# Buffers of the first weights' decoding moved off the first block's tiles, new planner costs, gates of the MLPs on two engines, and the first two blocks of the second MLP interleaved

## The chip, the cores and the metric

One core of one Trainium2 chip runs the whole program. The metric is the device time of one execution in microseconds (us), taken as the median of several runs. A profiled execution has a time of its own; the trace gives the span of that execution from its first to its last instruction.

## The reference

A recurrent attention layer (four batches, eight heads, 768 positions, head size 40), and two MLPs on its output, all in float32:

```python
for t in range(S):
    y[:, :, t] = np.einsum('bhd,bhde->bhe', rt, state)
    Sa = np.einsum('bhde,bhe->bhd', state, at)
    state_decay = state * wt[:, :, None, :] - np.einsum('bhd,bhe->bhde', Sa, bt)
    state = state_decay + np.einsum('bhd,bhe->bhde', vt, kt)
...
x = attn_out.transpose(0, 2, 1, 3).reshape(3072, 320)
x = np.maximum(x @ w_in1, 0.0) ** 2 @ w_out1      # 320 -> 2048 -> 320
x = np.maximum(x @ w_in2, 0.0) ** 2 @ w_out2      # the same with other weights
```

The weights reach the program as 64-bit floating-point numbers, looked at as pairs of 32-bit words. The kernel makes of each a high and a low part in the matmul's own 32-bit type (fp32r), which is here called decoding.

## The kernel before, in words

The recurrence is computed in 24 units of 64 positions for two batches at a time (`NUT`), each in two chunks of 32. A unit has `keys`, `values` and, for two units together, `invert`: a triangular inverse by some 45 dependent VectorE instructions. Then comes `chain`, which carries the state through the two chunks, and `store_y`, which writes the output to the DRAM tile `ys`. Two units give the 256 tokens of one block, of which there are 12. `block1` takes block m through the first MLP and writes it to `x2a` and `x2b`; `block2` takes it through the second. Each MLP has 16 steps per block (`f`, 128 of the 2048 hidden columns): `in_step`, eight matmuls of 128x256 into `HB[i % 2]`; `gate`, which makes the squared positive part as a high part `m_h` and a rest `m_l`; and `out_step1` (eight matmuls of 128x256) or `out_step2` (six of 128x320). So a step is 16 matmuls in the first MLP and 14 in the second. Block m's input is loaded by `load_x` into `m_x` and split into `m_xh` and `m_xl`.

`decode_w1` decodes the first weights in 40 chunks while the first units run; `decode_w2` decodes the second ones in 36 chunks. The second weights have no room in SBUF before the attention's tiles are given back, so that their loads begin behind the attention and the decoding runs beside the first MLP's last blocks.

The tile `mm` is shared. `m_x` lies in its columns 0 to 767, the evacuation tiles in 768 to 1791, the gate's two tiles `m_r` in 1792 to 2303. Before, the six raw buffers of `decode_w1` (`raw1`) cover columns 0 to 3071, so they lie over all of these.

No order is written out by hand. Every instruction is recorded by `_Engine.__getattr__` (line 69, which is why all rows of the trace bear that line) and put in order by `_Plan.run`. That is a list scheduler with a cost for each instruction (`cost`, `array`, `pe_time`), a priority (`plan.prio`; smaller goes first) and, for some instructions, a choice of engine (`either`). What it emits is the order in which each engine and the SP queue, which issues all transfers, execute. The times in it are its own estimates and have no part in the profile. `BIAS` is how many of its nanoseconds VectorE leaves a piece of work to another engine that could do it. `P_D` is the priority of the decoding, beside units' own numbers 0 to 23; `LP` is that of the first chunks' loads.

The lines that the prediction's steps touch, as they are before:

```python
raw1 = [mm[:, o:o + 512] for o in range(0, 3072, 512)]
...
A.activation(out=gg, in_=h, func=AF.Relu)
A.activation(out=gg, in_=gg, func=AF.Square)
...
P_X, P_G, P_M, P_D = -100.0, -200.0, 1000.0, 2.7
```

`check_w`, recorded behind the second MLP's fourth block, reads one input array through two buffers with 16 long VectorE reductions, to see whether a general path is needed; that path stands behind a branch and isn't executed on these inputs.

Of the kernel before, what the change touches and what calls it, by code (L numbers as in the profile page):

```python
# [26 lines left out]
NF = 16  # L27
# [45 lines left out]
class _Plan:  # L73
# [65 lines left out]
    def cost(self, eng, op, outs, ins):  # L139
# [17 lines left out]
        if op in ("tensor_copy", "tensor_scalar") and not psum:  # L157
            n /= 2
# [89 lines left out]
    def array(self, ops):  # L248

        cycles, columns, tiles, mode = 0, 0.0, [], None  # L250
        for _, _, passes, outs, ins, _ in ops:
# [10 lines left out]
            if ins[0].dtype == F32R:  # L262
                cycles += max(n, 2 * m) + 6
                columns += n * m / 128
                tiles = []
                continue
# [53 lines left out]
    def run(self, until=None):  # L320
        while until is None or self.left.get(until, 0):
# [20 lines left out]
            if e == "DVE":  # L342
                keep = []
                while avail:
                    z = heapq.heappop(avail)
                    j = z[1]
                    if j in self.done:
                        continue
                    keep.append(z)
                    alts = self.tasks[j][0]  # L350
                    cost = alts[e][1]
                    if any(
                        max(self.free[o], self.ready[j][o], t) + alts[o][1] <= t + cost + BIAS for o in alts if o != e
                    ):
                        continue
                    i = j
                    keep.pop()
                    break
# [29 lines left out]
def rwkv7_two_mlp_kernel(  # L388
# [73 lines left out]
    raw1 = [mm[:, o:o + 512] for o in range(0, 3072, 512)]  # L462
    exp1 = [mm[:, o:o + 256] for o in range(3072, 4096, 256)]
# [390 lines left out]
    def decode_w1(w, win, win3, wout):  # L854
# [18 lines left out]
        for k, z in enumerate(chunks):  # L873
            plan.first = LP if k < 6 else None
            plan.prio = p0 + 0.01 * k
            decode_t(*z, raw1[k % 6], exp1[k % 4], rest1[k % 6], bank[4 + (k + 2) % 4])
# [124 lines left out]
    def gate(h, i):  # L1001
        gg, gh, gl = m_r[i % 2], m_h[i % NG], m_l[i % NG]
        A.activation(out=gg, in_=h, func=AF.Relu)
        A.activation(out=gg, in_=gg, func=AF.Square)
# [18 lines left out]
    P_X, P_G, P_M, P_D = -100.0, -200.0, 1000.0, 2.7  # L1023
# [71 lines left out]
    def block2(m, at, rows):  # L1095
        ob = obs[m % 2]
        plan.prio = P_X + m
        load_x(x2a[at].rearrange("p (k t) -> p k t", k=2), x2b[at])
        split_x(m_xh[m % 2], m_xl[m % 2])
        for f in range(NF):  # L1100
            i = m * NF + f
            j = NBLK * NF + i
# [5 lines left out]
            out_step2(w2, f, i, ob)  # L1108
        plan.prio = P_G + j
# [33 lines left out]
    for m in range(NBLK):  # L1143
        block2(m, m, lambda p, s: orow[p, s, m])
        if m == min(3, NBLK - 1):
# [48 lines left out]
    with tc.If(bad > 0):  # L1194
# [4 lines left out]
        with tc.For_i(0, NU) as q:  # L1199
            block1(0, q)  # L1200
            block2(0, q, lambda p, s: orow[p, s, bass.ds(q, 1)].rearrange("o t d -> (o t) d"))
# [80 lines left out]
```

## Time and profile before

| what | value |
|---|---|
| median of 3 runs | 1203.9 us (1201.52 to 1204.97) |
| profiled execution, its own time | 1209.43 us |
| its span | 1207.6 us |
| TensorE busy | 1104.0 us, 91% |
| VectorE, ScalarE, GpSimd busy | 805.9, 747.5, 388.2 us |
| mean granted TensorE clock | 0.955 of full speed |

The profiled execution is 5.5 us longer than the median of the runs, so a sum made against it is carried over to the median as a difference. Busy times are those of one engine; a busy TensorE (PE in the rows) may still run at half its clock. The clock's two levels are 1.2 and 2.4 GHz, and the column PEclk says which share of 2.4 GHz was granted in the mean.

### The profile page before, as it was taken

The page shows a single profiled execution, that of the slowest core. Times are in us where ns is not written, and L with a number is a line of the kernel's source. Part 1 is how long each engine was busy: PE and PEld are TensorE (multiplying, and loading weights), DVE is VectorE, ACT ScalarE, POOL GpSimd, SP SyncE. Part 2 cuts the span into 40 slices and gives each one's busy share as a digit, 9 for nine tenths or more (in the row PEclk, how much of TensorE's full clock was granted, in tenths as well). Part 3 has the DMA queues.
Part 4 walks back from the last instruction along what each step waited for, and adds up shares of the span by engine and source line. Part 5 has one row for each costly group of instructions (what it writes and reads, how often), then busy time and mean ns, then how long its engine had stood idle before and what let it go on. Part 6 is the DMA issues. An engine that isn't in the chain of part 4 may idle for free.

```text
span 1207.6 us, 43193 instructions
## 1 busy us (share of the span) xinstructions
PE 1104.0 (91%) x18096; PEld 1032.2 (85%) x18096; DVE 805.9 (67%) x1786; ACT 747.5 (62%) x2077; POOL 388.2 (32%) x443
## 2 busy tenths in 40 slices
PE   3888898998989998899899999999899999999996
PEld 2656787887878887798789899999899999999996
DVE  6887888789888978999798746666773232222221
ACT  4496554555565565556446468888666666666664
POOL 7544334223323332343224117776820000000000
PEclk9986789999998999999899999999899999999999
DMA  8555343155325515533451322332241010101000
GB/s 244 143 154 146 85 104 103 57 127 146 79 70 138 136 49 127 143 90 78 123 121 36 60 74 84 93 93 82 79 140 36 25 29 24 33 24 27 13 12 14
DMA packets 142239, 103.86 MB, mean 86 GB/s; under 512 B 98001, under 2 KB 110162, under 8 KB 142034
## 3 DMA queue, kind: packets, MB, share of 16 engines
q1 hardware_dynamic: 142034, 101.00, 31.5%
q8 instruction: 144, 2.36, 0.8%
q14 instruction: 61, 0.50, 0.1%
HBM read 82.88 MB, written 11.80 MB: 78 GB/s over the span
## 4 chain that ended last, share of the span: by engine, by line
PE 50%; DVE 7%; ACT 3%; issue 2%; DMA 1%; POOL 1%; SPq 1%; DVEq 0%; ACTq 0%; POOLq 0%
PE bank L69 50%; DVE mm L69 3%; DVE q L69 2%; ACT mm L69 1%; ACT q L69 1%; SPq L69 1%; DVE x L69 0%; DVE y L69 0%; DVE kt L69 0%; ACT m_h L69 0%; DMA v<-in_el_dram 0%; POOL kb L69 0%; DMA lk<-kt 0%; DVE p L69 0%; DMA mm<-in_win_dram 0%
## 5 line engine op out<-in xcount | busy, mean ns | idle before, releaser
L69 PE MATMUL bank<-m_xh,wi 128*128 128x256 f32 x1920 | 387.0, 286 | 9.7 <-ACT mm L69 5.4
L69 POOL TENSOR_TENSOR m_l<-mm,m_h 128x256 fp32r<-128x256 f32 x200 | 162.8, 816 | 546.3 <-ACT m_h L69 293.7
L69 PEld LDWEIGHTS bank<-m_xh,wi 128*128 128x128 f32 x1920 | 315.3, 193 | 13.2 <-ACT mm L69 6.0
L69 PE MATMUL bank<-m_xl,wi 128*128 128x256 f32 x1152 | 324.2, 285 | 1.8 <-POOL m_xl L69 1.8
L69 ACT ACTIVATE mm<-bank 128x256 f32<-128x256 f32 x384 | 146.2, 382 | 233.1 <-PE bank L69 214.3
L69 DVE TENSOR_TENSOR m_l<-mm,m_h 128x256 fp32r<-128x256 f32 x184 | 85.0, 462 | 217.6 <-ACT m_h L69 209.7
L69 PEld LDWEIGHTS bank<-m_xl,wi 128*128 128x128 f32 x1152 | 222.3, 193 | 2.3 <-POOL m_xl L69 2.3
L69 ACT ACTIVATE mm<-mm 128x256 f32<-128x256 f32 (+3 forms) x500 | 205.0, 423 | 30.6 <-POOL m_xl L69 14.8
L69 PE MATMUL bank<-m_h,wo 128*128 128x256 f32 x960 | 206.7, 297 | 0.1
L69 PE MATMUL bank<-wo,m_h 128*128 128x320 f32 x768 | 172.5, 311 | 1.7 <-ACT m_h L69 1.2
L69 PEld LDWEIGHTS bank<-m_h,wo 128*128 128x128 f32 x960 | 156.6, 192 | 10.0 <-issue 1.4
L69 PE MATMUL bank<-m_l,wo 128*128 128x256 f32 x576 | 156.6, 284 | 0.1
L69 ACT CAST m_h<-mm 128x256 fp32r<-128x256 f32 x359 | 145.1, 405 | 10.2 <-PE bank L69 1.9
L69 PEld LDWEIGHTS bank<-wo,m_h 128*128 128x128 f32 x768 | 125.7, 190 | 2.2 <-ACT m_h L69 1.4
L69 PE MATMUL bank<-wo,m_l 128*128 128x320 f32 x384 | 119.2, 310 | 1.0 <-POOL m_l L69 1.0
L69 DVE TENSOR_TENSOR mm<-mm 128x30 f32<-128x30 f32 (+9 forms) x317 | 106.0, 334 | 8.4 <-ACT wi L69 0.7
L69 PEld LDWEIGHTS bank<-m_l,wo 128*128 128x128 f32 x576 | 110.7, 192 | 0.5 <-POOL m_l L69 0.3
L69 DVE TENSOR_TENSOR q<-bank,cs 32x128 f32<-32x128 f32 (+1 forms) x240 | 87.7, 366 | 30.6 <-ACT q L69 22.2
L69 PE MATMUL bank<-q,lk 128*40 128x72 f32 x1536 | 63.7, 233 | 23.7 <-DVE q L69 10.6
L69 PEld LDWEIGHTS bank<-q,lk 128*40 128x40 f32 x1536 | 53.7, 120 | 31.7 <-ACT mm L69 9.9
L69 ACT COPY q<-bank 40x256 f32<-40x256 f32 (+1 forms) x168 | 54.6, 325 | 37.3 <-PE bank L69 33.6
L69 ACT ACTIVATE q<-bank 32x160 f32<-32x160 f32 x192 | 56.6, 295 | 27.3 <-PE bank L69 24.8
(135 smaller groups left out, 1633.1 us busy)
## 6 DMA issues: line engine op xcount, KB each, us to landing
kb<-in_el_dram SPq DMA_DIRECT2D x24, 512.0 KB
mm<-in_win_dram SPq DMA_DIRECT2D x30, 256.0 KB
a<-in_el_dram SPq DMA_DIRECT2D x24, 256.0 KB
v<-in_el_dram SPq DMA_DIRECT2D x24, 256.0 KB
r<-in_er_dram SPq DMA_DIRECT2D x24, 256.0 KB
lk<-kt SPq DMA_DIRECT2D x96, 64.0 KB
mm<-in_wr_dram SPq DMA_DIRECT2D x20, 260.0 KB
mm<-in_wout_dram SPq DMA_DIRECT2D x20, 256.0 KB
```

Of the source, the lines that this page charges most:

```text
L69: self.plan.op(self, op, lambda: getattr(self.real, op)(*args, **kw), outs, ins, kw)
```

## The change

Six things change together.

1. `raw1` has four buffers instead of six, at columns that leave `m_x` and `m_r` free, and `exp1` three instead of four. Accordingly four first chunks, not six, are loaded with the early priority `LP`.
2. `P_D` falls from 2.7 to 1.2, so the decoding ranks ahead of units 2 and 3.
3. The planner's costs of scans, transposes, uint32 instructions and fp32r matmuls rise, and while attention work is left VectorE leaves MLP work to other engines for four times `BIAS`.
4. Both instructions of the gate may go to ScalarE or VectorE. VectorE forms the square as the PSUM value times its positive part, so it reads the PSUM bank twice.
5. Blocks 0 and 1 of the second MLP are recorded together, block 1 five steps behind block 0 (`LAG`), instead of one after the other.
6. `finish2` is the old end of `block2` as a function.

```diff
-        if op in ("tensor_copy", "tensor_scalar") and not psum:
+        if op == "tensor_tensor_scan":
+            n *= 2.15
+        elif op == "transpose":
+            n = max(1.09 * n, 1.85 * min(n, 512))
+        elif o.dtype == U32:
+            n *= 1.2
+        elif op in ("tensor_copy", "tensor_scalar") and not psum:
             n /= 2
         return (64 + n) / 0.96
...
-                cycles += max(n, 2 * m) + 6
+                cycles += max(n, 2 * m) + 30
...
+                    bias = BIAS * (4 if self.tasks[j][3] != "att" and self.left.get("att", 0) else 1)
                     if any(
-                        max(self.free[o], self.ready[j][o], t) + alts[o][1] <= t + cost + BIAS for o in alts if o != e
+                        max(self.free[o], self.ready[j][o], t) + alts[o][1] <= t + cost + bias for o in alts if o != e
...
-    raw1 = [mm[:, o:o + 512] for o in range(0, 3072, 512)]
-    exp1 = [mm[:, o:o + 256] for o in range(3072, 4096, 256)]
+    raw1 = [mm[:, o:o + 512] for o in (768, 1280, 2304, 2816)]
+    exp1 = [mm[:, o:o + 256] for o in (3328, 3584, 3840)]
...
-            plan.first = LP if k < 6 else None
+            plan.first = LP if k < 4 else None
...
-            decode_t(*z, raw1[k % 6], exp1[k % 4], rest1[k % 6], bank[4 + (k + 2) % 4])
+            decode_t(*z, raw1[k % 4], exp1[k % 3], rest1[k % 6], bank[4 + (k + 2) % 4])
...
-        A.activation(out=gg, in_=h, func=AF.Relu)
-        A.activation(out=gg, in_=gg, func=AF.Square)
+        plan.either(
+            lambda: A.activation(out=gg, in_=h, func=AF.Relu),
+            lambda: V.tensor_scalar(out=gg, in0=h, scalar1=0.0, scalar2=None, op0=ALU.max),
+        )
+        plan.either(
+            lambda: A.activation(out=gg, in_=gg, func=AF.Square),
+            lambda: V.tensor_tensor(out=gg, in0=h, in1=gg, op=ALU.mult),
+        )
...
-    P_X, P_G, P_M, P_D = -100.0, -200.0, 1000.0, 2.7
+    P_X, P_G, P_M, P_D = -100.0, -200.0, 1000.0, 1.2
...
-    def block2(m, at, rows):
-        ob = obs[m % 2]
...
+    def blocks2(ms, ats, rows):
+        steps = sorted((f + LAG * k, m, f) for k, m in enumerate(ms) for f in range(NF))
+        for i, (_, m, f) in enumerate(steps):
+            if f == 0:
+                plan.prio = P_X + m
+                load_x(x2a[ats[m - ms[0]]].rearrange("p (k t) -> p k t", k=2), x2b[ats[m - ms[0]]])
+                split_x(m_xh[m % 2], m_xl[m % 2])
+            j = (NBLK + ms[0]) * NF + i
...
+            if f == NF - 1:
+                plan.prio = P_G + j
+                finish2(obs[m % 2], lambda p, s: rows(m, p, s))
...
-    for m in range(NBLK):
-        block2(m, m, lambda p, s: orow[p, s, m])
-        if m == min(3, NBLK - 1):
+    LAG = 5
+    lead = min(2, NBLK)
+    for ms in (range(lead), *([m] for m in range(lead, NBLK))):
+        blocks2(ms, ms, lambda m, p, s: orow[p, s, m])
+        if ms[0] == 3:
             check_w()
```

Three places of the new order bear on what follows. The first is the SP queue from the store of unit 1's output (`ys` from `y1`) onwards; `mm` from `ys` is the load of block 0's input, `mm` from `in_w...` a raw weight chunk, `kb1`, `v` and `lk1` belong to units 2 and 3. Before:

```order
L69 DMA ys_63<-y1_122 40x8x64 x2
L69 DMA kb1_99<-in_el_dram 128x1024
L69 DMA v_97<-in_el_dram 128x512
L69 DMA lk1_109<-kt_110 32x16x32 x4
L69 DMA mm_81<-in_wout1_dram 128x512
L69 DMA v_97<-in_el_dram 128x512
L69 DMA mm_81<-ys_63 128x2x256
L69 DMA mm_81<-ys_63 64x256 x2
```

And now:

```order
L69 DMA ys_63<-y1_122 40x8x64 x2
L69 DMA lk0_108<-kt_110 32x16x32 x2
L69 DMA mm_81<-in_wout1_dram 128x512
L69 DMA mm_81<-ys_63 128x2x256
L69 DMA mm_81<-ys_63 64x256 x2
L69 DMA v_97<-in_el_dram 128x512
L69 DMA kb1_99<-in_el_dram 128x1024
L69 DMA lk1_109<-kt_110 32x16x32
L69 DMA mm_81<-in_wout1_dram 128x4x128
```

The load of block 0's input has moved from behind the last weight chunk to a place ahead of the last six, and ahead of `kb1` and `v`.

The second is TensorE at its last state matmuls of the attention (`q` with `lk`); the matmul of `nid` with 512 columns clears the banks for the first output step of the ninth block (m = 8). Before:

```order
L69 MATMUL bank5_72<-m_xh0_83,wi3_1_126 128x256
L69 MATMUL bank5_72<-m_xl0_85,wi3_1_126 128x256
L69 MATMUL bank2_69<-q1_112,lk1_109 40x72 x8
L69 MATMUL bank1_68<-q1_112,lk1_109 40x72 x8
L69 MATMUL bank6_73<-nid_82 128x512
L69 MATMUL bank6_73<-m_h2_89,wo1_127 128x256 x2
```

And now:

```order
L69 MATMUL bank5_72<-m_xh0_83,wi3_1_126 128x256
L69 MATMUL bank5_72<-m_xl0_85,wi3_1_126 128x256
L69 MATMUL bank2_69<-q1_112,lk1_109 40x72 x8
L69 MATMUL bank1_68<-q1_112,lk1_109 40x72 x8
L69 MATMUL bank6_73<-m_h0_87,wo1_127 128x256 x2
L69 MATMUL bank6_73<-m_l0_90,wo1_127 128x256
```

Before, the clearing matmul stood right behind them; now it stands four output steps ahead. Counted over TensorE's whole order, 130 of the first MLP's 192 input steps stood ahead of the last state matmul, and 134 do now.

The third is TensorE in the second MLP's first steps. Block 0 sums into banks 0 and 1 from `m_xh0`, block 1 into banks 2 and 3 from `m_xh1`; `wi2`, `wi3_2` and `wo2` are the second weights. Before:

```order
L69 MATMUL bank0_67<-wo2_11705,m_h2_89 128x320 x2
L69 MATMUL bank0_67<-wo2_11705,m_l2_92 128x320
L69 MATMUL bank1_68<-wo2_11705,m_h2_89 128x320 x2
L69 MATMUL bank1_68<-wo2_11705,m_l2_92 128x320
L69 MATMUL bank4_71<-m_xh0_83,wi2_11703 128x256
L69 MATMUL bank4_71<-m_xl0_85,wi2_11703 128x256
```

And now:

```order
L69 MATMUL bank5_72<-m_xh0_83,wi3_2_11792 128x256
L69 MATMUL bank5_72<-m_xl0_85,wi3_2_11792 128x256
L69 MATMUL bank2_69<-wo2_11793,m_h0_87 128x320 x2
L69 MATMUL bank2_69<-wo2_11793,m_l0_90 128x320
L69 MATMUL bank3_70<-wo2_11793,m_h0_87 128x320 x2
L69 MATMUL bank3_70<-wo2_11793,m_l0_90 128x320
L69 MATMUL bank4_71<-m_xh1_84,wi2_11791 128x256
L69 MATMUL bank4_71<-m_xl1_86,wi2_11791 128x256
```

Steps of block 1, which use weights decoded five steps earlier, now stand between those of block 0.

## Rows read from the trace of the kernel before

**Rows 1.** The page: span of the profiled execution.

```profile
span 1207.6 us, 43193 instructions
```

**Rows 2.** Windows by stage: us from the start, busy time and count of each engine, granted clock.

```profile
0.00:145.00 145.00, 102.18 (x1665) 80.88 (x1666) 117.24 (x294) 87.62 (x249) 74.09 (x84) 0.85 0.58 159
145.00:690.00 545.00, 498.02 (x12176) 452.53 (x12174) 470.12 (x1067) 308.02 (x891) 176.53 (x201) 0.96 0.39 99
690.00:840.00 150.00, 149.34 (x1607) 146.03 (x1606) 89.07 (x176) 116.68 (x335) 89.42 (x105) 1.00 0.29 84
840.00:880.00 40.00, 35.94 (x235) 34.53 (x234) 28.20 (x47) 29.85 (x82) 29.05 (x33) 0.87 0.34 99
880.00:1198.00 318.00, 318.00 (x2420) 317.97 (x2419) 100.74 (x204) 204.94 (x521) 19.15 (x22) 1.00 0.12 31
```

**Rows 3.** Timeline of TensorE where the first MLP begins: start, length, idle before.

```profile
134.83 0.29 PE L69 MATMUL bank<-m_xl,nid 128*128 128x256 f32 x1
138.14 0.58 PE L69 MATMUL bank<-m_xh,wi 128*128 128x256 f32 x1 [3.02 <-ACT m_xh L69]
140.02 0.58 PE L69 MATMUL bank<-m_xl,wi 128*128 128x256 f32 x1 [1.30 <-POOL m_xl L69]
143.39 0.41 PE L69 MATMUL bank<-m_xh,wi 128*128 128x256 f32 x1
```

**Rows 4.** Timeline of the SP queue, first store and load of `ys` for block 0.

```profile
118.06 0.81 SPq L69 DMA_DIRECT2D ys<-y  x2
...
131.90 1.80 SPq L69 DMA_DIRECT2D mm<-ys  x3
```

**Rows 5.** Windows of 5 us where TensorE waits in the second MLP.

```profile
835.00:840.00 5.00, 4.42 (x37) 4.22 (x37) 2.80 (x7) 4.91 (x16) 3.26 (x4) 1.00 0.41 134
855.00:860.00 5.00, 4.87 (x38) 4.61 (x36) 4.83 (x8) 3.43 (x11) 4.43 (x6) 1.00 0.37 105
860.00:865.00 5.00, 2.36 (x10) 1.91 (x11) 4.13 (x7) 2.77 (x10) 4.24 (x6) 0.91 0.28 73
865.00:870.00 5.00, 3.71 (x15) 3.12 (x15) 4.86 (x9) 2.29 (x6) 3.87 (x5) 0.50 0.32 76
870.00:875.00 5.00, 5.00 (x27) 4.89 (x27) 2.88 (x5) 4.53 (x12) 4.48 (x5) 0.56 0.24 84
```

**Rows 6.** Timelines of SP, GpSimd and VectorE: first load and last parts of the second weights.

```profile
717.16 0.84 SPq L69 DMA_DIRECT2D mm<-in_win_dram  x2
...
867.80 0.86 POOL L69 TENSOR_TENSOR wi<-mm 128x256 fp32r<-128x256 f32 x1
...
875.62 1.03 DVE L69 TENSOR_TENSOR wo<-dt 128x320 fp32r<-128x320 f32 x1
```

**Rows 7.** Windows of 30 us with TensorE full, first and second MLP.

```profile
750.00:780.00 30.00, 30.00 (x258) 29.95 (x258) 17.00 (x30) 25.89 (x74) 23.99 (x28) 1.00 0.29 86
930.00:960.00 30.00, 30.00 (x230) 30.00 (x229) 8.40 (x17) 19.25 (x50) 1.92 (x2) 1.00 0.09 25
```

**Rows 8.** Groups by form: count, busy us, mean ns of one, idle before.

```profile
L69 ACT ACTIVATE mm<-bank 128x256 f32<-128x256 f32 x384 | 146.2, 382 | 233.1 <-PE bank L69 214.3 <-POOL m_l L69 14.3 <-POOL x L69 2.1
L69 DVE TENSOR_TENSOR m_l<-mm,m_h 128x256 fp32r<-128x256 f32 x184 | 85.0, 462 | 217.6 <-ACT m_h L69 209.7 <-POOL m_xl L69 4.0 <-PE bank L69 1.9
L69 POOL TENSOR_TENSOR m_l<-mm,m_h 128x256 fp32r<-128x256 f32 x200 | 162.8, 816 | 546.3 <-ACT m_h L69 293.7 <-DVE m_h L69 139.4 <-issue 64.2
L69 DVE CAST m_h<-mm 128x256 fp32r<-128x256 f32 x25 | 7.3, 292 | 9.7 <-ACT mm L69 9.3 <-issue 0.2
L69 DVE COPY mm<-bank 128x320 f32<-128x320 f32 x12 | 5.9, 492 | 16.2 <-PE bank L69 14.9 <-DMA mm<-x2b 1.3
L69 DVE TENSOR_TENSOR mm<-bank,mm 64x256 f32<-64x256 f32 x12 | 4.9, 408 | 4.1 <-ACT mm L69 4.0
L69 DVE TENSOR_TENSOR_SCAN mm<-mm,cs 128x520 f32<-128x520 f32 x20 | 25.6, 1279 | 0.2
L69 DVE TENSOR_REDUCE cs<-mm 128x1 f32<-128x960 f32 x8 | 8.9, 1148 | 2.9 <-DMA mm<-in_nat_dram 2.8
```

**Rows 9.** Timelines of VectorE and GpSimd: one VectorE form beside idle and beside busy GpSimd.

```profile
61.17 0.28 DVE L69 TENSOR_SCALAR mm<-mm 128x256 uint32<-128x256 uint32 x1
62.09 0.82 DVE L69 TENSOR_SCALAR mm<-mm 128x256 uint32<-128x256 uint32 x1
...
61.31 1.46 POOL L69 TENSOR_TENSOR m_xh<-mm 128x256 fp32r<-128x256 f32 x1 [1.32 <-DVE sp L69]
```

More of the change, by code (lines that the diff above doesn't have):

```diff
@@ L1093, in rwkv7_two_mlp_kernel @@
     obs = [bank[0:2], bank[2:4]]
-    def block2(m, at, rows):
-        ob = obs[m % 2]
[L1097 to L1102, printed above, removed]
+    def blocks2(ms, ats, rows):
[6 more added lines that the diff above has]
+            j = (NBLK + ms[0]) * NF + i
             plan.prio = P_M + j
@@ L1107, in block2, with finish2 @@
             plan.prio = P_M + j + 1.5
-            out_step2(w2, f, i, ob)
-        plan.prio = P_G + j
+            out_step2(w2, f, i, obs[m % 2])
+            if f == NF - 1:
+                plan.prio = P_G + j
+                finish2(obs[m % 2], lambda p, s: rows(m, p, s))
+    def finish2(ob, rows):
         for s in range(2):
@@ L1200, in rwkv7_two_mlp_kernel @@
             block1(0, q)
-            block2(0, q, lambda p, s: orow[p, s, bass.ds(q, 1)].rearrange("o t d -> (o t) d"))
+            blocks2([0], [q], lambda m, p, s: orow[p, s, bass.ds(q, 1)].rearrange("o t d -> (o t) d"))
             plan.run()
```

## The prediction

> **What bounds the kernel now.** I read the windows by stage first [rows 2]. From 880 us to 1198 us TensorE is busy 318.00 of 318.00 us at the full clock: nothing that another engine does there can shorten the run. The same holds nearly for 690 to 840 us (149.34 of 150.00). Whatever is to be won lies in the three other stretches. Until 145 us TensorE is busy 102.18 us at a clock of 0.85. From 145 to 690 us, attention beside the first MLP, it is busy 498.02 of 545 us at 0.96, so it idles 47 us; VectorE idles 75 us there (545 less 470.12), so neither is the bound alone and the two wait for each other in turn. From 840 to 880 us TensorE is busy 35.94 of 40 at 0.87.
>
> TensorE's total work is fixed, and the second MLP ends the run. So the change can be counted in one currency: how many microseconds of MLP matmuls are already done when a stage ends, and how long TensorE then waits for weights. A step costs, by the full windows [rows 7], 16 matmuls x 30 us / 258 = 1.86 us in the first MLP and 14 x 30 / 230 = 1.83 us in the second.
>
> **The start of the first MLP.** I looked next at TensorE where the decoding ends [rows 3]. The last decoding matmul is issued at 134.83 us. The first input matmul begins at 138.14, after 3.02 us of waiting for the high part of block 0's input, and the next at 140.02, after 1.30 us for the rest. From 140.02 to 143.39 us 15 of these matmuls start, 0.225 us each, against 30 / 258 = 0.116 us in a full window: after its waits the engine runs at the lower of its two clock levels. The reason is in the SP queue [rows 4]: unit 1's output was stored at 118.06 us, but the load of block 0's input was issued at 131.90, because `m_x` lies under raw buffers that the last chunks still use. After the change that load stands ahead of the last six chunks, so the input can be split while they are decoded, and both waits should go: 3.02 + 1.30 = 4.3 us, and 15 x 0.109 = 1.6 us of half clock. That is 5.9 us of TensorE.
>
> The new order says how much of this the planner thinks it can use: four more first-MLP steps stand ahead of the attention's last state matmul (134 against 130), 4 x 1.86 = 7.4 us. If the attention ends when it did, the run is shorter by that; if TensorE is what the attention waits for, the attention ends 7.4 us later and nothing is won. I take 5.9, the waits that I can name, between bounds of 0 and 7.4. The decoding itself does not end sooner: counted in VectorE's order, 102 of its 120 decoding instructions stood ahead of unit 1's last output, now 92, and in both orders all 120 stand ahead of the inverse's second transpose. "Ahead of units 2 and 3" is paid for by fewer raw buffers.
>
> On VectorE the attention stretch changes little. It gains 12 positive parts, 5 products and 10 copies, and loses 6 rests, 6 of the inverse's first products, 2 input splits, 2 gate casts and a few others. Priced by the nearest rows [rows 8], 27 x about 0.41 us = 11 us come and about as much goes; the 75 us of idle hide the difference, 1 us if that cover is gone. GpSimd takes over 14 rests of 0.816 us and some larger pieces, about 20 us, against 368 us of idle there.
>
> The load moved ahead on SP must wait until `ys` is written, and `v` and `kb1` of unit 3 are queued behind it. Its own issue took 1.80 us; that delays unit 3 by 0 to 1.8 us, of which I take 0.5, since the weight chunk ahead of it waits for a buffer as well.
>
> **The second weights.** TensorE's losses here are in the 5 us windows [rows 5]: idle 0.58 + 0.13 + 2.64 + 1.29 = 4.6 us, and half clock 2.36 x 0.09 + 3.71 x 0.50 + 5.00 x 0.44 = 4.3 us, together 8.9 us. Their cause: the second weights are loaded from 717.16 us, when the attention gives its room back, and their last part is written at 876.65 us [rows 6], 159.5 us later; block 0's last step needs it sooner. In the order before, 62 first-MLP steps and 15 steps of block 0 are done ahead of that step: 62 x 1.86 + 15 x 1.83 = 143 us. Its input weights were ready 151.5 us after the first load (868.66) and its output weights after 159.5.
>
> After the change 58 steps remain, which makes it worse by 7.4 us, but with the lag of five, 25 second-MLP steps lie ahead: 58 x 1.86 + 25 x 1.83 = 153.6 us for the input weights, ready at 151.5; the output weights are wanted about two steps later, at 157.3, and ready at 159.5. So if the decoding keeps its pace a wait of about 2 us is left, and block 1's input steps can fill part of it. I keep 2.5 us of loss with its clock, and gain 8.9 - 2.5 = 6.4 us. Bounds: 8.9 if the decoding gains on it, 0 if the decoding slows by 7 us more.
>
> **The gates.** In the second MLP behind the decoding VectorE gets some 105 of the positive parts and as many squares. The trace of before has neither. For the positive part the nearest rows are the bank copies, 492 ns at 320 columns, and the cast at 292; for the product 408 [rows 8]. I take 0.42 each, 0.84 us against two ScalarE instructions near 0.38 to 0.42. The work is hidden: VectorE was busy 100.74 of 318 us [rows 2], and 105 x (0.84 + 0.29) = 119 us more still leaves a third idle. If the cover went, each gate could hold TensorE by the longer hold of its PSUM bank, 0.4 us, 42 us in all; below nothing is excluded, since TensorE has no idle left to give back. I take 0.
>
> One place is less safe. `check_w` puts 16 reductions of 1.148 us [rows 8] into VectorE's queue, with waits for their transfers, and now gates of blocks 2 to 4 stand behind them. If each held TensorE for its length it would cost 18.4 us; if the three gate buffers cover them, 0. I take 1.5, one reduction and a transfer's rest.
>
> **The sum.** -5.9 + 0.5 - 6.4 + 1.5 = -10.3 us. The profiled execution took 1209.4 us (span 1207.6 [rows 1] and 1.8 around it), so 1199.1 for one like it; that execution was 5.5 us above the median of the runs, so the median should be 1203.9 - 10.3 = 1193.6 us.
>
> **Rivals.**
>
> *Only one of the two terms pays* (0.20). The attention ends later by the steps that it took in, or the decoding falls behind as GpSimd serves more gates: with the two costs of 0.5 and 1.5, 1203.9 - 6.4 + 2 = 1199.5 or 1203.9 - 5.9 + 2 = 1200.0.
>
> *The attention itself shortens* (0.10). The planner charged a scan of 520 columns (64 + 520) / 0.96 = 608 ns; it measures 1279 [rows 8], and the new cost gives 1231. An order made with costs near the chip's should leave fewer moments where an engine's queue stands behind one late instruction. If a quarter of TensorE's 47 us of idle went as well, the time would be 1193.6 - 12 = 1181.6. Against it: the order of the middle units is hardly changed.
>
> *GpSimd holds VectorE up* (0.09). One uint32 instruction takes 0.28 us on VectorE, and 0.82 when it starts inside a GpSimd instruction that runs from 61.31 to 62.77 [rows 9]. The 20 us that GpSimd takes over in the attention could hold VectorE as long; with 10 of them on the path the gain is gone and the time is 1203.9; from 14 on it would be slower, and with all 20 it is 1193.6 + 20 = 1213.6. Against it: VectorE idles 75 us there, and it hands the pieces over. (The Trainium skill, page "SBUF — State Buffer", section "SBUF: two separate sides", says that VectorE and GpSimd share one pair of ports which either holds for a whole instruction while the other is blocked; the two rows agree, and by that rule alone each piece moved to GpSimd would be a risk and not a relief.)
>
> *The gates hold TensorE up* (0.11): slower. A gate now reads its bank twice, and VectorE also has sums, copies and reductions in one queue. From 880 us TensorE has no slack, so each wait is lost. To end slower the 105 gates must cost more than 10.3 + 3.6 = 13.9 us, 0.13 us each; at 0.2 us the time is 1193.6 + 21 = 1214.6. Against it: before, 22 rests of 0.816 us ran on GpSimd in that stretch [rows 2, 8], each longer by 0.35 than on VectorE, and TensorE was not held once.
>
> **How the numbers follow.** The forecast has 0.50, its own range 1187 to 1200. No change is within 0.3% of 1203.9, about what this measurement can tell: 1200.3 to 1207.5. Faster: 0.50, 0.15 of the first rival and 0.10 of the second, 0.75. Same: 0.05 of the first and the third (held up by 7 to 14 us), 0.14 in all. Slower: the gates, 0.11. The range of 1182 to 1206 leaves out the gates and half of the second rival.
>
> **What would show it.** Right: TensorE goes from decoding to block 0 with under 1 us of wait near 135 us; the first load of second weights is issued near 717 us; no 5 us window after it is below 0.9 of the full clock; behind the decoding TensorE is full. Wrong: the attention ends 5 us or more later; TensorE idles over 3 us behind 880 us beside VectorE's reductions or gates; the last second weights are written more than 165 us after their first load.

## The result: slower, by 0.6%

The changed kernel took 1211.2 us (median of 20 runs, 1204.7 to 1220.5) against 1204.3 us (20 runs) for the kernel before beside it. The ratio is 1.0057, interval [1.003, 1.0083]. The forecast of 1193.6 us and its range up to 1206 missed it. Slow runs are left out of all ratios and mean clocks; among the changed kernels that touches two of the twelve runs of *e1*, whose median holds all twelve.

The profiled execution of the changed kernel took 1219.37 us, 8.2 above its median; that of before was 5.5 above. So the two profiles differ by 10 us where the medians differ by 7. The page gives its span:

```profile
span 1217.8 us, 43019 instructions
```

The windows by stage of the changed kernel, columns as in [rows 2]:

```profile
0.00:145.00 145.00, 96.51 (x1600) 73.37 (x1600) 113.65 (x275) 84.37 (x237) 69.32 (x80) 0.80 0.58 157
145.00:690.00 545.00, 498.55 (x11780) 455.38 (x11778) 451.16 (x1037) 300.16 (x859) 192.65 (x222) 0.94 0.39 97
690.00:840.00 150.00, 148.23 (x1951) 142.91 (x1952) 93.77 (x209) 107.49 (x306) 74.08 (x87) 1.00 0.28 78
840.00:880.00 40.00, 37.77 (x298) 37.24 (x296) 22.13 (x44) 33.00 (x93) 28.63 (x34) 1.00 0.25 77
880.00:1198.00 318.00, 315.55 (x2388) 314.01 (x2389) 213.18 (x473) 98.30 (x250) 65.59 (x83) 1.00 0.15 41
```

Against [rows 2], 840 to 880 us is better (37.77 at the full clock for 35.94 at 0.87). The first two rows are worse: the granted clock is 0.80 for 0.85 and 0.94 for 0.96. In the second, TensorE idles as long as before (46.4 us for 47.0). Finer windows show where its clock fell, before and then after:

```profile
300.00:450.00 150.00, 136.25 (x3240) 124.77 (x3242) 130.70 (x307) 86.43 (x250) 49.42 (x57) 0.98 0.38 97
450.00:600.00 150.00, 137.60 (x3578) 124.24 (x3576) 134.60 (x291) 85.04 (x246) 49.00 (x55) 0.95 0.44 113
600.00:690.00 90.00, 83.93 (x1916) 76.30 (x1912) 76.75 (x195) 51.88 (x150) 24.07 (x30) 0.97 0.30 70
...
300.00:450.00 150.00, 138.31 (x3262) 127.04 (x3254) 128.53 (x287) 89.17 (x254) 58.05 (x68) 1.00 0.40 101
450.00:600.00 150.00, 139.39 (x3246) 127.30 (x3243) 126.03 (x299) 81.70 (x237) 46.28 (x55) 0.92 0.41 101
600.00:690.00 90.00, 81.57 (x1877) 74.12 (x1871) 67.91 (x158) 46.21 (x134) 28.68 (x33) 0.87 0.31 79
```

From 450 to 690 us TensorE is busy as long as before (220.96 us for 221.53), but its granted clock is 0.92 and 0.87 instead of 0.95 and 0.97. So about 150 x 0.03 + 90 x 0.10 = 13.5 us more of the full clock were not granted there, an estimate from columns of two digits.

**The start.** TensorE where the decoding gives way to the first MLP, from its timeline:

```profile
135.48 1.22 PE L69 MATMUL bank<-mm,cs 128*128 128x256 f32 x2 [2.66 <-DVE mm L69]
145.21 0.41 PE L69 MATMUL bank<-m_xh,nid 128*128 128x256 f32 x1
146.22 0.58 PE L69 MATMUL bank<-m_xh,wi 128*128 128x256 f32 x1 [0.59 <-ACT wo L69]
146.60 0.41 PE L69 MATMUL bank<-m_xl,wi 128*128 128x256 f32 x1
...
149.16 0.41 PE L69 MATMUL bank<-m_xl,nid 128*128 128x256 f32 x1
```

The waits of [rows 3] for block 0's input are gone. But the first input matmul begins at 146.22 us and not at 138.14, because the decoding is late: its last matmul is issued at 149.16 us, behind the first input matmuls, where [rows 3] have 134.83. The timelines of SP, ScalarE and VectorE show what it waited for:

```profile
123.13 1.64 SPq L69 DMA_DIRECT2D mm<-ys  x3
...
131.11 2.11 SPq L69 DMA_DIRECT2D mm<-in_win_dram  x1
...
134.14 1.27 ACT L69 ACTIVATE mm<-mm 128x256 f32<-128x256 f32 x3 [3.21 <-DMA mm<-in_wout_dram]
...
128.72 0.28 DVE L69 TENSOR_TENSOR sp<-sp 128x120 f32<-128x120 f32 x1
134.61 0.29 DVE L69 TENSOR_SCALAR mm<-mm 128x256 uint32<-128x256 uint32 x1 [5.60 <-ACT mm L69]
134.82 0.28 DVE L69 TENSOR_TENSOR sp<-sp 128x120 f32<-128x120 f32 x1
...
151.47 1.14 DVE L69 STREAM_TRANSPOSE tt<-sp 128x512 f32<-128x512 f32 x1
```

VectorE before, at the same places of the inverse:

```profile
128.65 0.28 DVE L69 TENSOR_TENSOR sp<-sp 128x120 f32<-128x120 f32 x1
...
142.83 1.10 DVE L69 STREAM_TRANSPOSE tt<-sp 128x512 f32<-128x512 f32 x1
```

Block 0's input is loaded 8.8 us earlier than in [rows 4]. But VectorE, in the middle of the inverse's chain (`sp`), has a decoding instruction next in its queue; that waits 5.60 us for ScalarE, and ScalarE for a raw weight chunk. The inverse stands still behind it. At 128.7 us the two kernels are level; the transpose that ends this second inverse starts at 151.47 us instead of 142.83. Most of the rest of the 8.6 us are decoding instructions that now stand between the inverse's last ones.

**The second weights.** First load and last part, from the timelines of SP and GpSimd, and the three poorest of the 5 us windows:

```profile
738.61 0.89 SPq L69 DMA_DIRECT2D mm<-in_win_dram  x2
...
905.70 1.07 POOL L69 TENSOR_TENSOR wo<-dt 128x320 fp32r<-128x320 f32 x1
...
875.00:880.00 5.00, 3.36 (x26) 3.09 (x24) 2.88 (x5) 2.97 (x9) 3.77 (x6) 1.00 0.01 3
895.00:900.00 5.00, 4.37 (x33) 4.06 (x32) 5.00 (x6) 2.51 (x7) 4.92 (x6) 1.00 0.04 8
900.00:905.00 5.00, 4.53 (x36) 4.37 (x34) 3.79 (x5) 4.58 (x12) 3.69 (x5) 1.00 0.49 122
```

The first load comes 21.5 us later than in [rows 6], because the attention ends later: its last state matmul ends at 737.46 us, before at 715.95. The decoding takes 168.2 us instead of 159.5. TensorE idles 2.23 us from 840 to 880 and 2.45 behind it, 4.7 us, all at the full clock, where [rows 5] had 8.9 us of idle and half clock.

**The second MLP.** One of the 30 us windows behind the decoding:

```profile
1110.00:1140.00 30.00, 30.00 (x231) 30.00 (x230) 18.94 (x46) 7.41 (x19) 4.20 (x6) 1.00 0.10 25
```

TensorE is as full as in [rows 7], with VectorE at 63%. The gates do not hold it up here.

**The account.** The attention's last state matmuls, before and after:

```profile
714.75 1.20 PE L69 MATMUL bank<-q,lk 128*40 128x72 f32 x32
...
736.26 1.20 PE L69 MATMUL bank<-q,lk 128*40 128x72 f32 x32
```

The attention ends 21.5 us later with four more steps done, worth 7.4: a loss of 14.1 us. The second weights give 8.9 - 4.7 = 4.2 back. 14.1 - 4.2 = 9.9 us; the spans differ by 10.2.

Where the 14.1 us arise can be read at the transposes that end the inverses, by the same sum: the time, less 1.86 us for each first-MLP step done by then (16 matmul records in the trace are a step). At the second inverse the kernel after owes 8.6 us more than before. But this delay is made up later. The transposes of the eighth inverse, before and after:

```profile
467.06 1.00 DVE L69 STREAM_TRANSPOSE tt<-mm 128x512 f32<-128x512 f32 x1
...
471.10 1.09 DVE L69 STREAM_TRANSPOSE tt<-mm 128x512 f32<-128x512 f32 x1
```

By then 1190 matmuls are done before and 1216 after, so 4.0 - 26 / 16 x 1.86 = 1.0 us is left of the delay. At the eleventh inverse (646.93 us with 1802 matmuls, 669.02 with 1872) it is 14.0. So this execution lost its time between 467 and 669 us, where the clock was lower, and not at the start.

I use this number below as the *debt* of an order: the time at which the last state matmul ends, less 1.86 us for each first-MLP step ahead of it in TensorE's order.

### The profile page after: what moved, and what is told of

Read it like the earlier page. It is cut to its first block, busy times and chain, and to the rows that moved or that the text cites. A ratio compares the mean times of both kernels' runs of the same rounds, so it can differ in the third digit from the quotient of the medians.

```text
span 1217.8 us, 43019 instructions
## 1 busy us (share of the span) xinstructions
PE 1108.2 (91%) x18096; PEld 1034.2 (85%) x18096; DVE 901.1 (74%) x2052; ACT 625.9 (51%) x1748; POOL 431.7 (35%) x506
## 5 line engine op out<-in xcount | busy, mean ns | idle before, releaser
L69 POOL TENSOR_TENSOR m_l<-mm,m_h 128x256 fp32r<-128x256 f32 x240 | 186.5, 778 | 540.9 <-ACT m_h L69 223.1
L69 ACT ACTIVATE mm<-bank 128x256 f32<-128x256 f32 x264 | 100.7, 382 | 317.2 <-PE bank L69 302.8
L69 ACT ACTIVATE mm<-mm 128x256 f32<-128x256 f32 (+2 forms) x389 | 160.1, 424 | 43.4 <-DMA mm<-in_win_dram 10.8
L69 PEld LDWEIGHTS bank<-m_h,wo 128*128 128x128 f32 x960 | 157.8, 193 | 10.2 <-issue 0.8
L69 DVE TENSOR_TENSOR m_l<-mm,m_h 128x256 fp32r<-128x256 f32 x144 | 68.6, 476 | 70.2 <-ACT m_h L69 60.9
L69 ACT CAST m_h<-mm 128x256 fp32r<-128x256 f32 x276 | 111.3, 405 | 12.2 <-PE bank L69 5.0
L69 DVE TENSOR_TENSOR mm<-mm 128x30 f32<-128x30 f32 (+8 forms) x314 | 99.6, 317 | 7.7
L69 DVE TENSOR_SCALAR mm<-bank 128x256 f32<-128x256 f32 x120 | 51.0, 425 | 56.8 <-PE bank L69 56.0
L69 PEld LDWEIGHTS bank<-wo,m_l 128*128 128x128 f32 x384 | 72.1, 188 | 5.5 <-POOL m_l L69 4.9
```

The lines of the kernel that those rows point to most:

```text
L69: self.plan.op(self, op, lambda: getattr(self.real, op)(*args, **kw), outs, ins, kw)
```

## Experiments

The times are medians; each ratio is to the kernel before, run beside it (1203.6 to 1206.2 us in the four sittings). A ratio is an estimate of its own and can differ from the quotient of the two medians, most in *e1* (1.0015 for 1.005). "Before" and "after" are the two kernels.

### One part undone in the kernel after, one part alone in the kernel before

*e1_old_buffers*: the kernel after with the raw buffers and rank of before, and with its `exp1` and early loads.

```diff
-    raw1 = [mm[:, o:o + 512] for o in (768, 1280, 2304, 2816)]
+    raw1 = [mm[:, o:o + 512] for o in range(0, 3072, 512)]
...
-    P_X, P_G, P_M, P_D = -100.0, -200.0, 1000.0, 1.2
+    P_X, P_G, P_M, P_D = -100.0, -200.0, 1000.0, 2.7
```

> The changed kernel with the six raw buffers, four expansion buffers, six early loads and rank 2.7 of the kernel before; costs, gates and the interleaving as changed. Theory A: four raw buffers let the decoding of the first weights fall behind (its last matmul 145.2 instead of 134.8 us, the second inverse's transpose 151.5 instead of 142.8 us), and all that follows is about 8.6 us later. Then this kernel takes 1211 - 8 = 1203 us, the second transpose is near 143 us, and the ratio to before is 0.996 to 1.002. Rival B: the new costs order the middle units worse (151.5 to 697.6 us = 546 us between second and last inverse, against 533.4 before). Then it stays above 1207, ratio 1.003 or more, with 545 us between those transposes.

Measured 1209.6 us, ratio 1.0015 [0.9984, 1.0045]. It lies between the two expectations, and so does its second inverse's transpose (146.8 us). Taken alone it says that the buffers and rank are part of the loss; the orders without content at the end of this section differ by more than that. Without buffers and rank the kernel is no faster than before, though it keeps the interleaving.

*e2_only_buffers*: the kernel before with these lines, and the smaller `exp1` and early loads, of the kernel after.

```diff
-    raw1 = [mm[:, o:o + 512] for o in range(0, 3072, 512)]
+    raw1 = [mm[:, o:o + 512] for o in (768, 1280, 2304, 2816)]
...
-    P_X, P_G, P_M, P_D = -100.0, -200.0, 1000.0, 2.7
+    P_X, P_G, P_M, P_D = -100.0, -200.0, 1000.0, 1.2
```

> The kernel before with the buffers, the early loads and the rank 1.2 of the change alone. Theory A: second transpose 6 to 9 us later than 142.8, and 1204 + 8 = 1212 us, ratio 1.004 to 1.009. Rival B: within 0.3% of before, ratio 0.997 to 1.003.

Measured 1223.4 us, ratio 1.0151 [1.0115, 1.0188], more than either theory gave.

*e3_only_lag*: the kernel before with the interleaving alone (item 5 of the change).

```diff
...
-    for m in range(NBLK):
-        block2(m, m, lambda p, s: orow[p, s, m])
+    LAG = 5
+    lead = min(2, NBLK)
+    for ms in (range(lead), *([m] for m in range(lead, NBLK))):
+        blocks2(ms, ms, lambda m, p, s: orow[p, s, m])
```

> The kernel before with the interleaving of the second MLP's first two blocks alone. If TensorE's losses at the second weights (8.9 us before) are the lag's to win: 1204 - 5 = 1199 us, ratio 0.994 to 0.998, no half clock between 840 and 900 us. If the decoding only moves its waits: ratio 0.999 to 1.002, and idle of 4 us or more between 840 and 920.

Measured **1196.3 us, ratio 0.9931 [0.9903, 0.9959]**, the fastest kernel of the study. Its window:

```profile
840.00:880.00 40.00, 40.00 (x304) 39.66 (x303) 29.57 (x44) 32.27 (x87) 32.87 (x38) 1.00 0.30 89
```

The loss of [rows 5] is wholly gone: 40.00 of 40 at the full clock. TensorE's order is that of before up to its 9361st instruction, and the last state matmul is its 8276th; so this part leaves the attention's order alone.

*e4_gate_scalar*: the kernel after with the gate on ScalarE only.

```diff
-        plan.either(
-            lambda: A.activation(out=gg, in_=h, func=AF.Relu),
-            lambda: V.tensor_scalar(out=gg, in0=h, scalar1=0.0, scalar2=None, op0=ALU.max),
-        )
+        A.activation(out=gg, in_=h, func=AF.Relu)
...
```

> The changed kernel with both instructions of the gate on ScalarE again. Rival C, that gates on VectorE hold TensorE up: 1211 - 4 = 1207 us or less, TensorE idle under 0.5 us behind 920 us and less of it from 870 to 910. Theory A, that the gates cost nothing: within 0.3% of the changed kernel, 1208 to 1214 us.

Measured 1216.8 us, ratio 1.0104 [1.0075, 1.0132]: 5.6 us slower than the kernel after, not faster. Its TensorE idles 4.45 us from 880 to 920 us, where the kernel after has 2.45, and not at all behind 920. So that idle time is not the doing of gates on VectorE. The time is above either expectation, and the 5.6 us are less than the 10 us by which orders of the kernel after differ (below).

### The other parts alone, and combined with the interleaving

*e8_lag_gate*: the kernel before with the interleaving and the gate on two engines (the `plan.either` lines above put in).

> The kernel before with the interleaving of blocks 0 and 1 and with the gate on two engines, and its own raw buffers, rank and planner costs. The interleaving alone measured 0.9931, and taking VectorE out of the gate made the changed kernel 5.6 us slower (1216.84 against 1211.2). If the two gains are separate they add up: 1203.6 - 7.3 - 5.6 = 1191 us, ratio 0.988 to 0.992. If the gate gains only because the changed kernel's decoding and order leave ScalarE late, it adds nothing here: 1195 to 1198, ratio 0.993 to 0.996.

Measured 1207.7 us, ratio 1.0025 [1.0002, 1.0048]. Both expectations missed: the same edit that gained 5.6 us in the kernel after loses 11.4 us here. A cost of the gate itself would hardly have both signs. The debt is 483.1 against 468.4 for the interleaving alone: the loss lies in the attention, where the planner dealt another order and some gates moved to VectorE.

*e9_only_costs*: the kernel before with item 3 of the change.

```diff
+        if op == "tensor_tensor_scan":
+            n *= 2.15
...
-                cycles += max(n, 2 * m) + 6
+                cycles += max(n, 2 * m) + 30
...
```

> The kernel before with the planner's new costs and its fourfold bias alone. The changed kernel with the old buffers measured 1.0015, though it has the interleaving (0.9931) and the gates on two engines (about 0.995); so if the parts add up, the costs alone lose about 1.2%: 1214 to 1220 us, with the attention's last inverse transposes later than 676 us by 8 or more. Rival: the parts don't add up and costs alone change nothing, 1200 to 1207. The prediction's own second rival (truer costs shorten the attention by 12 us) would give 1192.

Measured 1226.8 us, ratio 1.0185 [1.0154, 1.0215], slower than all three expectations.

*e10_only_rank*: the kernel before with `P_D` at 1.2.

> The kernel before with the rank of the decoding at 1.2 instead of 2.7 alone; six raw buffers. Buffers and rank together measured 1.0151. If the rank does it (units 2 and 3 are held back by decoding work that nobody yet waits for), 1214 to 1222 us. If the fewer buffers do it, the rank alone is 1200 to 1207, with the last decoding matmul at or before 135 us.

Measured 1211.7 us, ratio 1.0073 [1.0049, 1.0097]. Its timeline of TensorE:

```profile
127.33 0.28 PE L69 MATMUL bank<-m_xl,nid 128*128 128x256 f32 x1
...
130.09 0.39 PE L69 MATMUL bank<-m_xh,wi 128*128 128x256 f32 x1 [0.93 <-ACT m_xh L69]
131.98 0.39 PE L69 MATMUL bank<-m_xl,wi 128*128 128x256 f32 x1 [1.50 <-POOL m_xl L69]
```

With six raw buffers the rank does bring the decoding forward: its last matmul is issued at 127.33 us for 134.83 in [rows 3], and the first input matmul begins 8 us earlier. Part of this can be the execution: in *e3*, which has the order of before there, it begins at 134.06. The two waits for block 0's input are still there (0.93 and 1.50 us).

*e11_only_four*: the kernel before with the buffer lines of *e2* and the old rank.

> The kernel before with four raw buffers, three expansion buffers and four early loads alone; the rank stays at 2.7. If the fewer buffers do it (each of 40 chunks waits longer for a load, since a buffer comes free only when its chunk is decoded), 1214 to 1222 us and the last decoding matmul at 145 us or later. If the rank does it, 1200 to 1208, and less still if the earlier load of block 0's input pays its 5.9 us: 1198.

Measured 1221.3 us, ratio 1.0145 [1.0121, 1.0169]. The last decoding matmul lies at 148.7 us, as expected, though the inverse's second transpose is late by only 0.8 us against the profile of before. Most of the loss comes later: TensorE idles 54.3 us from 145 to 690 us, behind the decoding.

*e14_lag_rank*: the interleaving and the rank.

> The kernel before with the interleaving and the rank of 1.2. The rank alone measured 1.0073, but its trace shows the first MLP begin at 130 us instead of 138, the attention end at 709 us instead of 716, and then a longer wait for the second weights (33.5 us busy of 40 from 840 to 880, against 35.9). If the rank's whole loss is that wait, the interleaving takes it away: 1190 to 1197 us, ratio 0.989 to 0.995. If the rank's loss lies in the attention, it adds to the interleaving's 0.9931: 1203 to 1207, ratio 0.999 to 1.002.

Measured 1202.1 us, ratio 0.9964 [0.9943, 0.9985], above the first expectation and below the second. The wait from 840 to 880 us is gone (39.87 busy); with the rank the interleaved kernel is 0.3%, 4 us, slower than without.

*e5_old_costs*: the kernel after with the costs of before.

> The changed kernel with the planner's old costs and bias; four raw buffers, rank 1.2, gates on two engines and interleaving stay. The costs alone made the kernel before slower by 1.85%. If that is a cost of the new numbers as such, taking them out gives 1189 to 1200 us. If parts don't add up because each of them only deals the order anew (theory R), 1203 to 1215, near the changed kernel's own 1211.

Measured 1211.6 us, ratio 1.0038 [1.001, 1.0065], no clear difference from the kernel after (1.0057), although these costs alone had lost 1.85%. Parts that don't add up, whatever their sign, asked for an experiment with no part at all.

### Changes that mean nothing

Each of these alters one number of the planner's costs by 1 to 3 of its units. No work, buffer, rank or engine choice is edited, only the order comes out another, and with it the engine that the planner picks for a few gate pieces (at most 11 of the 384 rests move).

```diff
-                cycles += max(n, 2 * m) + 6
+                cycles += max(n, 2 * m) + 7
```

> The kernel before with one number of the planner changed that means nothing: 7 instead of 6 in the cost of a matmul. No work, buffer, rank or engine choice is edited; only the order that the planner deals is another one, from about TensorE's 1880th instruction on. So far every one of four different edits to the kernel before that touches the attention's order made it slower (costs 1.0185, four buffers 1.0145, rank 1.0073, gate 1.0094 on top of the interleaving), and the one that does not touch it did not. Theory R (the order before is a good draw, and any other deal loses): 1208 to 1220 us, with the debt per pair of blocks above the 63 us of before. Rival S (each edit has a cost of its own): 1200 to 1207.

```diff
-        return (64 + n) / 0.96
+        return (65 + n) / 0.96
```

> The same with another number that means nothing: 65 instead of 64 in the cost of a VectorE instruction. 133 instead of 130 input steps of the first MLP stand ahead of the attention's last state matmul. Theory R: 1208 to 1220 us. Rival S: 1200 to 1207.

```diff
-            return (55 if psum else 93) + (90 if len(ins) > 1 else 0) + n / 1.2
+            return (55 if psum else 95) + (90 if len(ins) > 1 else 0) + n / 1.2
```

> The kernel before with 95 instead of 93 in the planner's cost of a ScalarE instruction that reads SBUF: a third order dealt without meaning. If the order before is a good draw, 1207 to 1218 us (the first two such kernels measured 1.0044 and 1.0071). If those two were bad luck, 1199 to 1206. A draw above 1.0145 would mean that the four buffers (1.0145) and the costs (1.0185) need no cause of their own.

```diff
-            return 149 + 2.1 * n if ins else 35 + 0.83 * n
+            return 152 + 2.1 * n if ins else 35 + 0.83 * n
```

> The same with 152 instead of 149 in the cost of a GpSimd instruction: a fourth order without meaning. The same numbers: 1207 to 1218 us if the order before is a good draw, 1199 to 1206 if not; above 1.0145 the buffers and costs need no cause of their own.

And on the kernel after:

```diff
-                cycles += max(n, 2 * m) + 30
+                cycles += max(n, 2 * m) + 31
```

> The changed kernel with 31 instead of 30 in the cost of a matmul, which means nothing. If the changed kernel is itself one draw among its orders, this one differs from it by some us either way, between 1200 and 1218 us. If its loss is the work and waits of the edits, it is within 0.3% of it: 1208 to 1215.

```diff
-        return (64 + n) / 0.96
+        return (65 + n) / 0.96
```

> The changed kernel with 65 instead of 64 in the cost of a VectorE instruction. The same: 1200 to 1218 us, and not where the kernel before it lies, if the order is drawn; 1208 to 1215 if the loss belongs to the edits themselves.

| kernel | median, us | ratio to before | attention ends, us | steps ahead | debt, us | execution less median, us |
|---|---|---|---|---|---|---|
| before | 1203.6 to 1206.2 | 1 | 715.95 | 130 | 474.2 | +5.5 |
| before, PE cost 7 | 1212.7 | 1.0044 [1.002, 1.0069] | 717.33 | 131 | 473.7 | -2.5 |
| before, DVE cost 65 | 1216.6 | 1.0071 [1.0046, 1.0096] | 731.30 | 133 | 483.9 | +6.6 |
| before, ACT cost 95 | 1216.8 | 1.0098 [1.0066, 1.0129] | 718.46 | 130 | 476.7 | +0.6 |
| before, POOL cost 152 | 1224.2 | 1.0160 [1.013, 1.019] | 726.69 | 133 | 479.3 | -1.1 |
| after | 1211.2 | 1.0057 [1.003, 1.0083] | 737.46 | 134 | 488.2 | +8.2 |
| after, PE cost 31 | 1205.8 | 1.0007 [0.9982, 1.0031] | 719.76 | 132 | 474.2 | -0.4 |
| after, DVE cost 65 | 1216.6 | 1.0092 [1.0058, 1.0126] | 725.82 | 133 | 478.4 | -7.6 |

The last four columns are of one profiled execution each, the steps counted in the order. All four meaningless orders on the kernel before are slower, by 0.4% to 1.6%, 0.9% in the mean: three within what was expected of a good draw, POOL cost 152 above it. The three orders of the kernel after lie 0.85% apart, 10 us, and both new ones outside the 1208 to 1215 us that a loss of the edits themselves would give.

An execution that takes longer than its kernel's median has part of that in its debt. Before and *e3* have one order up to the attention's end; their debts are 474.2 and 468.4, and their executions lie 5.5 us above and 1.0 below their medians. *e10* and *e14* also share theirs: 467.1 and 473.8, 5.9 and 1.2 us below. With the last column taken off, each pair agrees within 2 us. By that estimate the four meaningless orders owe 7 to 12 us more than before, and the three of the kernel after 6 to 17.

One pair shows it without such a correction. The order of PE cost 7 is that of before, and of *e3*, up to about 224 us. At the third inverse, ahead of that, its execution and that of *e3* are level (213.69 and 214.24 us, 311 matmuls done in both); at the end of the attention its debt is 5.3 us larger. What differs between the two is the order behind 224 us and the engines picked in it. From one execution to another of one order there is less: from the third inverse to the end the distance of before and *e3* goes from 6.7 to 5.8 us.

Where the debt in the table is near that of before (PE cost 7, ACT cost 95), the wait for the second weights is longer: from 840 to 880 us TensorE is busy 34.51 and 32.31 us, for 35.94. The worst of the first four, in its windows by stage:

```profile
145.00:690.00 545.00, 487.86 (x11951) 443.65 (x11950) 462.61 (x1047) 303.97 (x874) 178.72 (x197) 0.96 0.39 98
...
840.00:880.00 40.00, 33.71 (x208) 30.20 (x207) 33.23 (x48) 28.37 (x80) 33.16 (x39) 0.83 0.34 94
```

TensorE idles 57.1 us in the attention, for 47.0 in [rows 2], at the same clock. The first MLP has 59 steps left to cover the second weights with instead of 62, and the wait for these grows too. The best order of the kernel after:

```profile
145.00:690.00 545.00, 502.00 (x12183) 457.30 (x12184) 474.09 (x1081) 307.22 (x882) 198.25 (x221) 0.96 0.40 99
```

It idles 43.0 us, less than the kernel before. The edits that moved the decoding are all in it, and its second inverse is as late as in the kernel after (152.53 us).

## Why the prediction was wrong

**The step that failed** is the price of the attention: "On VectorE the attention stretch changes little." The sum has no term for it; 1 us was named for the case that no idle time hid the difference. In the profiled execution the attention ended 21.5 us later with four more steps done, a loss of 14.1 us, and all but 1.0 of it arose behind the eighth inverse, in the units whose order the forecast called "hardly changed". The price was made by exchanging instructions that come for instructions that go. But what the planner emits is not the old order with some pieces exchanged. A change that it sees ahead of the attention can deal the order of all later units anew, and the runs with no content show what that alone does on the kernel before: +0.4% to +1.6%, 5 to 19 us. The change's +0.6% holds the interleaving, which alone gains 0.7% and leaves the attention's order as it was; if that gain adds, all that touches the attention loses about 1.3%, inside that span.

**The second step that failed** is the start, -5.9 us. The mechanism named for it came: block 0's input is loaded 8.8 us earlier, and the waits of 3.02 and 1.30 us are gone, in the kernel after and in all other kernels with four raw buffers. What failed is that the decoding was taken to end when it did. Its last matmul is issued at 131.5 to 137.3 us in the profiles of before and its four meaningless orders; with four raw buffers at 140.7 to 150.2 (seven kernels), with six and the new costs at 141.7 (*e9*) and 143.3 (*e1*), and with six and the rank at 127.3 and 128.2 (*e10*, *e14*). So the rank brings the decoding forward, and the fewer buffers and the new costs each put it back by more than another order alone does. The forecast named the fewer buffers as the price of the rank, and put that price, like the costs', at nothing.

The longest single wait, the 5.60 us of VectorE at 134.61 us, takes both in the runs at hand (none has the new costs and the rank with six buffers): it is there in all four kernels with four buffers and the new costs (5.60, 4.71 in *e4*, 3.79 and 3.09 us in the two meaningless ones); with six buffers no wait of VectorE for a chunk reaches 1 us there, and with four buffers and the old costs 1.06 us is the longest (*e2*). The gain of 5.9 us was lost by this. The delay itself, 8.6 us, was made up again by the eighth inverse (1.0 left; 0.7 in *e4*, -1.3 and -2.6 in the two meaningless ones). That the forecast and the result differ by so much is therefore not the start's doing alone. What made the delay up I don't know.

**The four extra steps** ahead of the attention's end (134 for 130) were held to be worth 0 to 7.4 us. They were worth nothing by themselves: the attention ended 21.5 us later. The prediction's alternative, that the attention ends later by what it takes in, covered a third of this. The first and the last of its signs of being wrong both came: an attention that ends 5 us or more later, and 168.2 us, over 165, for the second weights.

**The second weights, -6.4 us.** The mechanism was right, and alone so was the size: -7.3 us for the interleaving. In the change it gave less, 8.9 - 4.7 = 4.2 us of TensorE's time in the kernel after, which has fewer steps left to cover the decoding with and whose decoding took 8.7 us longer. The forecast's lower bound ("0 if the decoding slows by 7 us more") was too low for that. The sum's other term, 1.5 us for `check_w`, is not seen: TensorE idles 0.26 us in all behind 905 us.

**The gates, 0.** Right where it was forecast: TensorE is full behind the decoding. The rival that the gates hold it up falls by the same rows, and *e4* does not bring it back.

**The other rivals.** "Only one of the two terms pays" is what became of the terms: the second weights gave 4.2 us and the start nothing. But at 1199.5 us that was still faster than before; only the rival of GpSimd holding VectorE up let the attention grow by more than it took in, and it was given no chance of ending slower. That truer costs shorten the attention is refuted in this kernel: alone they lose 1.85%, and taking them out of the kernel after changes nothing (1.0038 against 1.0057). GpSimd holding VectorE up had no run of its own, but the traces speak against it: from 145 to 690 us GpSimd is busy 192.65 us for 176.53, yet VectorE's instructions there, 1006 of forms that both kernels have, take 1.9 us less in all than they would at each form's mean length before. And the best order of the kernel after has still more GpSimd work (198.25 us).

**What stays open.** The costs alone (1.0185) lie above what the four meaningless changes did (up to 1.0160 [1.013, 1.019]), the four buffers alone (1.0145) near its upper end. At the start both have an effect of their own; with four draws I can't say whether they have one on the time. Nor do I know what makes the order before better than its neighbours, or why the order of the kernel after is granted a lower clock behind 450 us. It is not the same in all: the kernel after lost by the clock, POOL cost 152 by idle time.

## What to carry to other kernels

Where a list scheduler deals the order, an edit ahead of a stage in which two engines wait for each other costs or gains what its new order does there, and no row of the trace before shows that: give it a term of its own, with the spread that meaningless changes of a cost number measure. Read off where the loss arises before blaming the first late instruction: here a delay of 8.6 us was made up, and the loss came 300 us later and more. Run such a change beside each part of a real one before giving a part credit or blame. An edit that the order shows to leave the hard stage untouched, as the interleaving does, can be priced from the trace, and alone came out within 2 us of its term (-7.3 us for -6.4).

## What the runs showed that I had not expected

The same order can take different times. The kernel before and the one with the interleaving share it up to the attention's end, yet in their profiled executions that end lies at 715.95 and 710.19 us; 3.6 us of the difference are there by the inverse's second transpose (142.83 and 139.20), with a granted clock of 0.85 and 0.88 until 145 us.

And a short idle time can be followed by a much longer stretch at the lower clock. In the kernel after, by 5 us windows:

```profile
560.00:565.00 5.00, 3.09 (x57) 2.88 (x58) 4.67 (x13) 3.27 (x10) 2.54 (x2) 1.00 0.00 0
565.00:570.00 5.00, 5.00 (x119) 4.43 (x117) 4.33 (x15) 3.58 (x11) 0.72 (x1) 1.00 0.17 47
...
595.00:600.00 5.00, 5.00 (x102) 4.64 (x100) 4.68 (x14) 2.04 (x8) 0.74 (x1) 1.00 0.55 114
600.00:605.00 5.00, 3.43 (x170) 2.85 (x164) 4.61 (x7) 3.54 (x11) 2.27 (x2) 0.97 0.64 130
605.00:610.00 5.00, 4.91 (x140) 4.36 (x144) 3.18 (x5) 1.91 (x6) 1.30 (x2) 0.50 0.43 120
610.00:615.00 5.00, 4.70 (x124) 3.87 (x115) 1.66 (x5) 1.96 (x6) 0.00 (x0) 0.50 0.51 163
615.00:620.00 5.00, 4.49 (x83) 4.01 (x83) 3.01 (x6) 0.79 (x3) 2.33 (x2) 0.50 0.02 3
```

TensorE idled 1.57 us between 600 and 605, and then ran 15 us at 0.50, the lower level, though it was busy 14.1 of them. It is no rule: between 560 and 565 it idled 1.91 us and kept the full clock. The 13.5 us of clock that the kernel after lost between 450 and 690 us are made of such stretches, so the same idle time in another order can cost more.

It is not only this execution, which took 8.2 us more than the median. Over all its runs the kernel after was granted 0.952 of the clock in the mean, the kernel before 0.959 to 0.960 in the four sittings, the interleaving alone 0.963, and the costs alone, the slowest, 0.943. But the clock is not all: the four buffers alone had 0.955 and were slower than the kernel after.
